# The S1·T1 product of a down projection by a second level of Strassen, with its right sums sharing a buffer through DRAM

## The chip, the cores and the metric

The kernel runs on one core of one Trainium2 chip. The metric is the device time of the whole program in microseconds, and the profile is one execution of it. TensorE (PE in the profile) does the matmuls, VectorE (DVE) the elementwise sums, ScalarE (ACT) copies, exponentials and the GELU, and SyncE (SP) issues the DMAs.

## The reference

Two blocks stand one after the other. The first is a cross attention between `x` (8 batches, 8 heads, 512 rows, 64 deep) and a `state` of 32 rows, in both directions. Its result is 544 rows of 512 numbers for each batch. The second is a two-layer net with a sigmoid GELU:

```python
scores = scale * x @ state.T;  a = softmax(scores);   xread = a @ state      # 512 rows
scores2 = scale * state @ x.T; a2 = softmax(scores2); sread = a2 @ x         # 32 rows
h = concat(xread, sread) @ w_in          # 512 -> 2048
g = h * sigmoid(1.702 * h)
return g @ w_out                          # 2048 -> 512
```

All is fp32.

## The kernel before, in words

**Batches and stages.** The 512 rows of xread are worked off batch by batch (b = 0 to 7). The 32 rows of sread of all batches come last, as one piece called "sr". Batch 0 uses plain matmuls. For b = 1 to 7 the down projection `g @ w_out` is done in `strassen_two(b, ...)`, and while it runs, the attention of batch b+1 is put between its products. That is done with hooks: `strassen_two` calls `hook("P2a")`, `hook("P6.3")` and so on at named points, and a dictionary says which pieces of other work are emitted there. Instructions are emitted by hand (`manual_schedule`), and every engine runs its own in the order of emission.

**The down projection.** `g` (512 tokens by 2048) and `w_out` (2048 by 512) are cut in halves in both directions and multiplied in seven products (Winograd's form of Strassen) in the order P1 = A11·B11, P2 = A12·B21, P5 = S1·T1, P6 = S2·T2, P3 = (A12−S2)·B22, P7 = S3·T3, P4 = A22·T4. The S are sums of quarters of `g`, and the T sums of quarters of `w_out`, made once. S1 and S2 lie in the tile `later`, T1, T2 and T4 in `sums`, T3 in place in `w_out`. One product is 256 tokens × 1024 × 256. Written plainly (`product` in `strassen_two`) it is 16 matmuls of 128×128 weights against 256 columns. An fp32 matmul shows as two records, so a product is 32 records.

**The second level.** Some of the seven are themselves done in seven products of quarters, by `strassen_low`: 7 products of 4 matmuls against 128 columns, 56 records. Before the change these are P6 and P7 (b = 1 to 7) and P4 (b = 2 to 7). `strassen_low` takes turns over three PSUM banks (`bank`, used as o[0], o[1], o[2], o[0], o[1], o[2], o[0]). After each product the result is added by DVE (the first copied by ACT) into `pu` or the target `R`, and `at(i)` lets other work in. A product can begin only when the instruction that emptied its bank is done. One bank is always `bank_o[1]`, where P2 is collected too. After P2, DVE empties `bank_o[1]` into `osb`, the output tile of the first quarter.

**What the second level needs.** On the right are three sums of quarters of T: `low2` and `low3` (for T2 and T3) lie in the tile `low`, those of T4 in DRAM, and are loaded into the x buffer each batch (`low4_load`). A further quarter of T is replaced in place (`low_third`). On the left are three sums of quarters of S and one replaced in place; for P6 these are three DVE instructions of 128×512 and a fourth (q1, q2, q4 and the line with `whole(1, 0)`).

**Buffers and helpers that the change touches.** `att_M(b, c)` computes a product of state and w_in, tile M of batch b, chunk c, and the four M tiles of a batch come from a pool with four turns. `up_sums(b)` makes sums of M for the up projection (`up_strassen`), which is called before P1 of the same batch and ends inside it. `att_s_norm` normalizes the second softmax. In the last batch (b = 7) there is no attention to prepare, so `sr_sums()` puts its DVE sums of w_in in the hooks instead: its `order` names how many at which hook.

Of the kernel before, what the change touches and what calls it, by code (L numbers as in the profile page):

```python
# [20 lines left out]
def kernel(  # L21
# [55 lines left out]
    konst = ctx.enter_context(tc.tile_pool(name="konst", bufs=1))  # L77
    xpool = ctx.enter_context(tc.tile_pool(name="xpool", bufs=1))
    apool = ctx.enter_context(tc.tile_pool(name="apool", bufs=1))
    mpool = ctx.enter_context(tc.tile_pool(name="mpool", bufs=4))  # L80
    gpool = ctx.enter_context(tc.tile_pool(name="gpool", bufs=1))
    opool = ctx.enter_context(tc.tile_pool(name="opool", bufs=1))
    dram = ctx.enter_context(tc.tile_pool(name="dram", bufs=1, space=bass.MemoryType.DRAM))
# [261 lines left out]
    def att_s_exp(b, room=None):  # L345
# [4 lines left out]
        for g in range(NG):  # L350
# [2 lines left out]
            nc.scalar.activation(out=e, in_=a["s"][g], func=AF.Exp, bias=a["mx2"][g], scale=scale, accum_out=sm)  # L353
            a["e2"].append((e, sm))

    def att_s_norm(b):

        for e, sm in A[b]["e2"]:
            nc.vector.tensor_scalar(sm, sm, eps, None, ALU.add)
            nc.vector.reciprocal(out=sm, in_=sm)  # L360
            nc.vector.tensor_scalar(e, e, sm, None, ALU.mult)

    NS1 = NG * NB

# [53 lines left out]
    def x_back(b, g):  # L418
# [2 lines left out]
            a["aT"] = apool.tile([P, NG, S], FP32, tag="aT", name=f"aT_{b}")  # L421
        nc.vector.transpose(a["aT"][:, g], a["e1"][:, g].rearrange("p i n -> p (i n)"))

    def att_M(b, c, spare=False):

        m = mpool.tile([P, NG, FC], FP32, tag="M", name=f"M_{b}_{c}")
        A[b]["M", c] = m
        name = f"M_{b}_{c}_"
        ps = [psH.tile([P, FC], FP32, tag="h", name=name + str(g)) if spare else att_ps([P, FC], name + str(g)) for g in range(NG)]
        by_state(b, ps, lambda rows, j: w_in[c][rows, j])  # L430
        for g in range(NG):
            nc.scalar.copy(m[:, g], ps[g])  # L432
# [150 lines left out]
    low2, low3 = ([low[:, 3 * i + k].rearrange("p (f n) -> p f n", f=QF) for k in range(3)] for i in range(2))  # L583


    kept4 = dram.tile([P, 3 * FC], FP32, name="low4")

    def low4_room():
        t = xpool.tile([P, SCH, H, D], FP32, tag="xn", name="low4")
        return t.rearrange("p c h d -> p (c h d)")[:, : 3 * FC]  # L590

    def low4_parts(t):
        return [t[:, FC * k : FC * (k + 1)].rearrange("p (f n) -> p f n", f=QF) for k in range(3)]

    def low4_make(a):
        t = low4_room()
        for fn, args in low_sums(T4, low4_parts(t)):
            fn(*args)
        nc.sync.dma_start(kept4, t)

    def low4_load(a):
        a["low4"] = low4_room()
        nc.sync.dma_start(a["low4"], kept4)

    def halves_of(t):

# [49 lines left out]

    def strassen_two(key, dst, hooks, a4):

        B11, B21, B22 = w_out[:, :HF, :HN], w_out[:, HF:, :HN], w_out[:, HF:, HN:]
        g = [G[key, u] for u in range(HF)]  # L660
        half = S // 2
# [30 lines left out]
            return [bank_o[1], *(psH.tile([P, FC], FP32, tag="h", name=f"low_{key}") for _ in range(2))]  # L692


        q1, q2, q4 = (g[i][:, :, :half].rearrange("p k (h t) -> p k h t", h=2) for i in range(3))
        v1, v2, v4 = (later[:, 1 + i].rearrange("p (k h t) -> p k h t", k=2, h=2) for i in range(3))
        k1 = g[3][:, :, :half]
        k2, k3, t01, o10, o01 = (room(i) for i in (0, 4, 5, 6, 7))
        z11, z12, z21, z22 = ([S2[:, QF * k + f, P * i : P * (i + 1)] for f in range(QF)] for i in range(2) for k in range(2))

        def whole(i, k):
            return S2[:, QF * k : QF * (k + 1), P * i : P * (i + 1)].rearrange("p (k h) t -> p k h t", h=2)

        def blocks(q):
            return [q[:, f // 2, f % 2] for f in range(QF)]

        product(bank(0), A_of(0, 0), B11, "P1")
        nc.scalar.copy(k1, bank(0))
        tt(q1, whole(1, 0), whole(1, 1))
        tt(q2, q1, whole(0, 0), ALU.subtract)  # L710
        tt(q4, whole(0, 1), q2, ALU.subtract)
        product(bank(1), A_of(0, 1), B21, "P2")
        osb = opool.tile([P, 2, HN], FP32, tag="osb", name=f"osb_{key}_00")
        tt(osb, bank(1), k1)
# [3 lines left out]
            a12 = quarters(key, NU + u, S)[0]  # L718
            tt(a12, a12, S2[:, 2 * u : 2 * u + 2, :half], ALU.subtract)

        for u in range(NU // 2):
            s4(u)
        tt(whole(1, 0), whole(0, 0), whole(1, 0), ALU.subtract)
        hook("P2")
        for u in range(NU // 2, NU):
            s4(u)
        hook("S4")
        product(bank(0), [S1[:, f, :half] for f in range(HF)], T1, "P5")
        b11, t3, b21, b22 = halves_of(T2)
        strassen_low(  # L730
            (z11, z12, z21, z22, blocks(q1), blocks(q2), blocks(q4)), (b11, t3, b21, b22, *low2),
            low_banks(), k2, lambda i: hook(f"P6.{i}"),
        )
        tt(k2, k2, k1)

        def sums(u0, rooms):

# [14 lines left out]
            return parts(0, 0), parts(1, 0), parts(0, 1), parts(1, 1), *(blocks(v) for v in rooms)  # L752

        left3 = sums(0, (v1, v2, v4))
        tt(t01, bank(0), k2)
        hook("P6")
        if a4 is not None:
            left4 = sums(NU, (q1, q2, q4))
        product(bank(3), A_of(0, 1), B22, "P3")
        b11, t3, b21, b22 = halves_of(T3)  # L760
        o, h0, h1 = low_banks()
        strassen_low(left3, (b11, t3, b21, b22, *low3), [h0, h1, o], k3, lambda i: hook(f"P7.{i}"))
        hook("P7")
        osb = opool.tile([P, 2, HN], FP32, tag="osb", name=f"osb_{key}_11")
        then = [
            lambda: tt(k3, k3, k2),
            lambda: tt(osb, bank(0), k3),
            lambda: out(1, 1, osb),
            lambda: tt(o01, bank(3), t01),
            lambda: out(0, 1, o01),  # L770
        ]
        if a4 is not None:
            turn = {1: then[:1], 2: then[1:3], 3: then[3:]}

            def at(i):
                for fn in turn.get(i, ()):
                    fn()
                hook(f"P4.{i}")

            b11, t3, b21, b22 = halves_of(T4)  # L780
            o, h0, h1 = low_banks()
            strassen_low(left4, (b11, t3, b21, b22, *low4_parts(a4["low4"])), [o, h1, h0], k1, at)
            p4 = k1
        else:
            for fn in then:
                fn()
            product(bank(2), A_of(1, 1), T4, "P4")
            for i in range(1, 8):
                hook(f"P4.{i}")
            p4 = bank(2)  # L790
# [4 lines left out]
    def hooks_next(b):  # L795

        h = {}

        def at(name, fn, *args):
            h.setdefault(name, []).append((fn, args))  # L800

        at("P1a", att_state, b)
        at("P1a", att_xT, b, 0)
        at("P1b", att_xT, b, 1)
        at("P1b", att_xT, b, 2)
        at("P1b", att_xT, b, 3, True)
        at("P2a", att_scores, b)
        at("P2a", att_M, b, 0)
        at("P2a", att_M, b, 1, True)
        at("P2a", att_blocks, b)  # L810
        at("P2a", att_s_max, b)
        at("P2a", att_s_exp, b)
        for g in range(NG):
            at("P2a", x_max, b, g)
            at("P2a", x_sub, b, g)
        at("P2a", x_exp, b)
        at("P2", att_s_norm, b)
        for name, fn, *args in (
            ("P6.1", x_sum, 0), ("P6.2", x_sum, 1), ("P6.3", x_inverse), ("P6.4", x_scale, 0), ("P6.6", x_scale, 1),
        ):  # L820
            at(name, fn, b, *args)
        for g in range(NG):
            at("P6", att_eT, b, g)
            at("P6", x_back, b, g)
        at("P3a", att_sread, b)
        at("P3a", att_M, b, 3, True)
        at("P3a", att_M, b, 2)
        steps = up_sums(b)
        for name, n in (("P3a", 7), ("P7.1", 1), ("P7.2", 1), ("P7.3", 1), ("P7.4", 1), ("P7.6", 1), ("P4.4", 2), ("P4.6", 1)):
            for fn, args in steps[:n]:  # L830
                at(name, fn, *args)
            steps = steps[n:]
        assert not steps
        at("P3b", att_srT, b)
        return h
# [56 lines left out]
    def sr_sums():  # L892

        HT, HK = B * Ns // 2, NPR // 2
        mm = [mpool.tile([P, NG, FC], FP32, tag="M", name=f"ws_{i}") for i in range(4)]
        s1, s2 = mm[:2], mm[2:]
        t = apool.tile([P, NPR, S], FP32, tag="xT", name="ws4")
        s4 = [t[:, HK * c : HK * (c + 1)] for c in range(2)]
        t = apool.tile([P, NG, NB, Ns], FP32, tag="e1", name="ta_sr").rearrange("p g i n -> p (g i n)")
# [8 lines left out]

        steps = []
        for c in range(2):  # L910
            steps.append((tt, (s1[c], hi[c][0], hi[c][1], ALU.add)))
            steps.append((tt, (s2[c], s1[c], lo[c][0])))
            steps.append((tt, (hi[c][0], lo[c][0], hi[c][0])))
            steps.append((tt, (s4[c], lo[c][1], s2[c])))
        steps += [(tt, v) for v in ((t1, r12, r11), (t2, r22, t1), (t3, r22, r12), (t4, r21, t2))]

        def each(v):
# [206 lines left out]
    for b in range(1, B):  # L1124
        if b > 1:
            ahead = {"P1a": [(up_strassen(b, S, *parts_x(b)), ())]}
        else:
            ahead = {
                "P1a": low_sums(T2, low2) + [(T_of, (T4, B21, T2)), (low_third, (T2,))],
                "P1b": low_sums(T3, low3) + [(low_third, (T3,))],  # L1130
            }
        if b + 1 < B:
            hooks = hooks_next(b + 1)
        else:

            steps, left, right = sr_sums()
            order = (
                ("P1b", 1), ("P2a", 4), ("P2", 1), ("P5a", 1), ("P3a", 1), ("P7.1", 1), ("P7.2", 1), ("P7.3", 1), ("P7.4", 1),
            )
            hooks = {}  # L1140
            for name, n in order:
                hooks[name], steps = steps[:n], steps[n:]
            assert not steps
            for name, t in (("P6", T2), ("P4.1", T3), ("P4.7", T4)):
                hooks[name] = [(low_third, (t,))]
        for name, first in ahead.items():
            hooks[name] = first + hooks.get(name, [])
        a4 = {}
        k = 3 if b + 1 < B else 0
        hooks["P3a"][k:k] = [(low4_load if b > 1 else low4_make, (a4,))]  # L1150
        strassen_two(b, out_of(b), hooks, a4 if b > 1 else None)
        if b == 1:
            low_third(T4)
# [38 lines left out]
```

## Time and profile before

| | |
|---|---|
| time | 735.43 us (median of 3, 735.40 to 735.52) |
| span of the profiled execution | 733.5 us, granted TensorE clock 0.999 |
| PE busy | 720.7 us, 98% of the span |
| DVE busy | 539.5 us, 74% |
| ACT busy | 234.1 us, 32% |
| DMA | 40.84 MB, mean 56 GB/s |

Busy time is the time in which an engine had an instruction running. The chain of waits, followed back from the last instruction, runs over PE for 95% of the span. Batches 2 to 6 look the same in the timeline, one every 79.4 us. Batch 1 and batch 7 differ from them, because batch 1 also makes the T sums, and batch 7 prepares no attention.

### The profile page before, as it was taken

What the parts mean: (1) busy time and instruction counts of PE and PEld (TensorE: products, weight loads), DVE (VectorE), ACT (ScalarE), POOL (GpSimd) and SP (SyncE); (2) the same over time, 40 slices, a digit from 0 to 9 for tenths busy, and PEclk for the clock granted to TensorE, in tenths of its full rate; (3) what the DMA queues carried; (4) which work ended last, traced back from release to release, by engine and by line L of the source; (5) the groups of instructions that cost most, each with busy time, mean ns of one, the idle gap of its engine ahead of it and who ended that gap; (6) DMA issues with size and microseconds to landing.
All of it is one profiled execution on the core that took longest, in us unless ns stands there. A gap on an engine that the chain in (4) does not pass through costs nothing.

```text
span 733.5 us, 11513 instructions
## 1 busy us (share of the span) xinstructions
PE 720.7 (98%) x4759; PEld 567.5 (77%) x4759; DVE 539.5 (74%) x1077; ACT 234.1 (32%) x430; POOL 0.8 (0%) x8
## 2 busy tenths in 40 slices
PE   7999999999999999999999999999999999999996
PEld 3333444467888789879888789878987988899995
DVE  6998999729856887668867786688766886788440
ACT  4786411033224511433144322451143314300210
POOL 0000000000000000000000000000000000000000
PEclk9999999999999999999999999999999999999999
DMA  8931245010140001300140014001130011010000
GB/s 225 355 91 54 90 154 135 0 59 15 44 105 1 16 31 57 61 1 16 45 104 1 16 45 105 0 16 35 54 62 1 15 44 44 1 57 30 16 1 29
DMA packets 49780, 40.84 MB, mean 56 GB/s; under 512 B 36544, under 2 KB 44224, under 8 KB 49728
## 3 DMA queue, kind: packets, MB, share of 16 engines
q1 hardware_dynamic: 49728, 40.11, 18.7%
q8 instruction: 37, 0.61, 0.4%
q14 instruction: 15, 0.12, 0.1%
HBM read 30.41 MB, written 9.70 MB: 55 GB/s over the span
## 4 chain that ended last, share of the span: by engine, by line
PE 95%; ACT 2%; DMA 2%; SPq 0%; DVE 0%; issue 0%; DVEq 0%; ACTq 0%
PE o L676 28%; PE o L944 17%; PE low L628 11%; PE o L490 8%; PE h L472 7%; PE o L628 6%; PE upx L944 6%; PE M L303 4%; PE o L533 2%; PE xT L282 2%; PE o L303 1%; PE sr L452 1%; PE warm L123 1%; PE upx_sr L944 1%; DMA out_dram<-osb_sr 1%; PE eT L441 1%
## 5 line engine op out<-in xcount | busy, mean ns | idle before, releaser
L676 PE MATMUL o<-w_out,g 128*128 128x256 f32 x672 | 152.7, 381 | 0.0
L954 DVE TENSOR_TENSOR g<-o,g 128x512 f32<-128x512 f32 (+1 forms) x140 | 88.1, 651 | 85.3 <-PE o L944 84.4
L676 PEld LDWEIGHTS o<-w_out,g 128*128 128x128 f32 x672 | 125.2, 190 | 26.2 <-issue 10.5
L951 ACT ACTIVATE g<-g 128x512 f32<-128x512 f32 (+1 forms) x84 | 49.9, 601 | 100.5 <-DVE g L954 100.5
L676 PE MATMUL o<-sums,later 128*128 128x256 f32 x224 | 49.5, 379 | 0.0
L944 PE MATMUL upx<-aT,M 128*128 128x256 f32 x192 | 49.3, 379 | 0.0
L944 PE MATMUL o<-ta,M 128*128 128x256 f32 x192 | 49.3, 379 | 0.0
L944 PE MATMUL o<-ta,ms 128*128 128x256 f32 x192 | 48.3, 379 | 0.0
L676 PEld LDWEIGHTS o<-sums,later 128*128 128x128 f32 x224 | 42.6, 190 | 5.8
L432 ACT COPY M<-M 128x512 f32<-128x512 f32 x64 | 33.2, 596 | 37.7 <-PE M L303 37.7
L944 PEld LDWEIGHTS o<-ta,ms 128*128 128x128 f32 x192 | 36.5, 190 | 5.0
L944 PEld LDWEIGHTS o<-ta,M 128*128 128x128 f32 x192 | 36.5, 190 | 5.0
L944 PEld LDWEIGHTS upx<-aT,M 128*128 128x128 f32 x192 | 36.1, 190 | 4.7
L513 DVE TENSOR_TENSOR later<-g,g 128x512 f32<-128x512 f32 (+1 forms) x32 | 20.8, 650 | 17.5 <-ACT g L475 17.5
L303 PE MATMUL M<-w_in,stT 64*32 64x512 f32 x512 | 32.7, 594 | 0.2 <-ACT eT L442 0.2
L628 PE MATMUL low<-low,g 128*128 128x128 f32 x256 | 32.8, 275 | 0.0
L472 PE MATMUL h<-low,M 128*128 128x512 f32 x64 | 29.7, 600 | 1.4 <-DVE low L384 1.4
L628 PEld LDWEIGHTS low<-low,g 128*128 128x128 f32 x256 | 30.7, 192 | 0.0
L472 PE MATMUL h<-aT,M 128*128 128x512 f32 x64 | 28.7, 599 | 1.4 <-ACT M L432 1.4
L635 ACT COPY pu<-o 128x128 f32<-128x128 f32 x13 | 3.5, 266 | 82.6 <-PE o L628 82.6
L490 PE MATMUL o<-w_out,g 128*128 128x512 f32 x64 | 28.7, 594 | 0.0
L490 PE MATMUL o<-w_out,sums 128*128 128x512 f32 x64 | 28.4, 594 | 0.0
(186 smaller groups left out, 1169.7 us busy)
## 6 DMA issues: line engine op xcount, KB each, us to landing
later<-in_moe_w_out_dram SPq DMA_DIRECT2D x16, 512.0 KB
xn<-in_x_dram SPq DMA_DIRECT2D x28, 256.0 KB
w_out<-in_moe_w_in_dram SPq DMA_DIRECT2D x12, 512.0 KB
low<-low SPq DMA_DIRECT2D x7, 768.0 KB
out_dram<-osb SPq DMA_DIRECT2D x18, 256.0 KB
out_dram<-later SPq DMA_DIRECT2D x14, 256.0 KB
later<-in_moe_w_in_dram SPq DMA_DIRECT2D x4, 512.0 KB
sums<-in_x_dram SPq DMA_DIRECT2D x4, 256.0 KB
```

Of the source, the lines that this page charges most:

```text
L282: nc.tensor.transpose(ps[:, c], x_heads(b, c, j), ident)
L303: nc.tensor.matmul(ps[g][st], A[b]["stT"][rows, st], rhs(rows, j), start=True, stop=True)
L432: nc.scalar.copy(m[:, g], ps[g])
L472: nc.tensor.matmul(hps, lhs[i], rhs[i], start=(i == 0), stop=(i == n - 1))
L490: nc.tensor.matmul(ops, G[key, f // 2][:, f % 2, P * r : P * (r + 1)], w_out[:, f], start=(f == 0), stop=(f == NF - 1))
L513: nc.vector.tensor_tensor(out=s1, in0=a21, in1=a22, op=ALU.add)
L533: nc.tensor.matmul(ps[:, r], lhs[f][:, P * r : P * (r + 1)], rhs[:, f], start=(first and r == 0 and f == 0), stop=(f == HF - 1), skip_grou ...
L628: nc.tensor.matmul(ps, lhs[f], rhs[:, f], start=(f == 0), stop=(f == QF - 1))
L676: nc.tensor.matmul(ps[:, r], lhs[f][:, P * r : P * (r + 1)], rhs[:, f], start=(r == 0 and f == 0), stop=(f == HF - 1), skip_group_check=True,)
L944: nc.tensor.matmul(ps[:, k], lhs[i][:, o : o + P], rhs[i], start=(first and k == 0 and i == 0), stop=(i == n - 1), skip_group_check=True,)
L951: nc.scalar.activation(out=dst, in_=src, func=AF.Gelu_apprx_sigmoid)
L954: nc.vector.tensor_tensor(out=dst, in0=ps, in1=x, op=ALU.add)
```

## The change

P5 is done by `strassen_low` as well in batches 2 to 7, so that four of the seven products use the second level. Its purpose is fewer PE cycles: 7 products of quarters in place of 8. Where its operands go:

- Left sums of S1: three rooms in the M tiles of chunks 2 and 3 (`spare_M`). These are idle between the end of the up projection and `att_M(b+1, 3)`. The fourth room holds the result p5, which then lies in SBUF and not in PSUM bank 0. The M tiles get fixed places by chunk (tags M0 to M3), with one buffer each.
- Right sums of T1: the place of `low3` is shared. `low_keep` writes the sums of T3 to DRAM in batch 1, `low5_make` makes those of T1 in the spare M rooms (hook "S4" of batch 1) and writes them to DRAM. From then on `low_load(3)` follows P5 and `low_load(5)` follows P7.
- DVE work moves: the three sums and the replaced quarter of S1 stand before P2. `s4(0)`, `s4(1)` and the replaced quarter of S2 go into P5's `at(1)` to `at(3)`. The normalizations of the second softmax go to `at(4)` and `at(6)` of P5. `t01` is formed right after P6.
- `sr_sums` can't use the M tiles of chunks 2 and 3 now, so it uses the tiles aT and eT, and its sums are cut in two (16 of 128×512 in place of 8 of 128×1024, and 4 small ones as before), with a new `order`. For "sr", T1 is restored by `low_third` in batch 7, as T2, T3 and T4 are.

```diff
+    turns = {"M": 0}
-        m = mpool.tile([P, NG, FC], FP32, tag="M", name=f"M_{b}_{c}")
+        m = mpool.tile([P, NG, FC], FP32, tag=f"M{turns['M'] % NFC if b < 2 else c}", name=f"M_{b}_{c}")
...
+    def low_load(k):
+        nc.sync.dma_start(turn_room, outside[k])
...
+    def spare_M():
+        m = [mpool.tile([P, NG, FC], FP32, tag=f"M{i}", name="spare_M") for i in (2, 3)]
+        return [v[:, g] for v in m for g in range(NG)]
+    def low5_make():
+        rooms = spare_M()
+        for fn, args in low_sums(T1, [v.rearrange("p (f n) -> p f n", f=QF) for v in rooms[:3]]):
+            fn(*args)
...
         product(bank(0), A_of(0, 0), B11, "P1")
         nc.scalar.copy(k1, bank(0))
-        tt(q1, whole(1, 0), whole(1, 1))
-        tt(q2, q1, whole(0, 0), ALU.subtract)
-        tt(q4, whole(0, 1), q2, ALU.subtract)
+        sums_of(S2, q1, q2, q4)
+        if not plain:
+            *r, p5 = spare_M()
...
+            sums_of(S1, *r)
+            third_of(S1)
         product(bank(1), A_of(0, 1), B21, "P2")
         osb = opool.tile([P, 2, HN], FP32, tag="osb", name=f"osb_{key}_00")
         tt(osb, bank(1), k1)
         out(0, 0, osb)
...
-        for u in range(NU // 2):
-            s4(u)
-        tt(whole(1, 0), whole(0, 0), whole(1, 0), ALU.subtract)
         hook("P2")
+        first = [lambda: s4(0), lambda: s4(1), lambda: third_of(S2)]
...
+            strassen_low(left_of(S1, *r), (b11, t3, b21, b22, *low5), [h0, h1, o], p5, at)
+            low_load(3)
         for u in range(NU // 2, NU):
             s4(u)
         hook("S4")
-        product(bank(0), [S1[:, f, :half] for f in range(HF)], T1, "P5")
+        if plain:
+            p5 = bank(0)
+            product(p5, [S1[:, f, :half] for f in range(HF)], T1, "P5")
...
-            low_banks(), k2, lambda i: hook(f"P6.{i}"),
+            left_of(S2, q1, q2, q4), (b11, t3, b21, b22, *low2), [h1, o, h0], k2, lambda i: hook(f"P6.{i}")
         tt(k2, k2, k1)
+        tt(t01, p5, k2)
...
+        if key + 1 < B:
+            low_load(5)
...
+        if b > 2:
+            at("P5.4", s_norm, b, 0)
+            at("P5.6", s_norm, b, 1)
+        else:
+            at("P2", att_s_norm, b)
...
+                steps += [(tt, (out[:, k], x0[:, k], x1[:, k], *op)) for k in range(HK)]
...
-            order = (
-                ("P1b", 1), ("P2a", 4), ("P2", 1), ("P5a", 1), ("P3a", 1), ("P7.1", 1), ("P7.2", 1), ("P7.3", 1), ("P7.4", 1),
-            )
+            order = [("P1b", 2), ("P2a", 8)]
+            order += [(name, 1) for name in ("P5.4", "P5.6", "P6.1", "P6.3", "P6.4", "P6.6", "P7.1", "P7.2", "P7.3", "P7.4")]
...
-            for name, t in (("P6", T2), ("P4.1", T3), ("P4.7", T4)):
+            for name, t in (("P6.2", T1), ("P6", T2), ("P4.1", T3), ("P4.7", T4)):
```

More of the change, by code (lines that the diff above doesn't have):

```diff
@@ L79 @@
     apool = ctx.enter_context(tc.tile_pool(name="apool", bufs=1))
-    mpool = ctx.enter_context(tc.tile_pool(name="mpool", bufs=4))
+    mpool = ctx.enter_context(tc.tile_pool(name="mpool", bufs=1))
     gpool = ctx.enter_context(tc.tile_pool(name="gpool", bufs=1))
@@ L354, in att_s_exp, with s_norm @@
             a["e2"].append((e, sm))
+    def s_norm(b, g):
+        e, sm = A[b]["e2"][g]
+        nc.vector.tensor_scalar(sm, sm, eps, None, ALU.add)
+        nc.vector.reciprocal(out=sm, in_=sm)
+        nc.vector.tensor_scalar(e, e, sm, None, ALU.mult)
     def att_s_norm(b):
[L358 to L361, printed above, removed]
+        for g in range(NG):
+            s_norm(b, g)
     NS1 = NG * NB
@@ L422, in x_back @@
         nc.vector.transpose(a["aT"][:, g], a["e1"][:, g].rearrange("p i n -> p (i n)"))
+    turns = {"M": 0}
     def att_M(b, c, spare=False):
-        m = mpool.tile([P, NG, FC], FP32, tag="M", name=f"M_{b}_{c}")
+        m = mpool.tile([P, NG, FC], FP32, tag=f"M{turns['M'] % NFC if b < 2 else c}", name=f"M_{b}_{c}")
+        turns["M"] += 1
         A[b]["M", c] = m
@@ L583, with low_keep @@
     low2, low3 = ([low[:, 3 * i + k].rearrange("p (f n) -> p f n", f=QF) for k in range(3)] for i in range(2))
-    kept4 = dram.tile([P, 3 * FC], FP32, name="low4")
+    low5 = low3
+    outside = {k: dram.tile([P, 3 * FC], FP32, name=f"low_{k}") for k in (3, 4, 5)}
+    turn_room = low[:, 3:].rearrange("p k n -> p (k n)")
+    def low_load(k):
+        nc.sync.dma_start(turn_room, outside[k])
+    def low_keep(k, src):
+        nc.sync.dma_start(outside[k], src)
     def low4_room():
@@ L590, in low4_room, with low_parts @@
         return t.rearrange("p c h d -> p (c h d)")[:, : 3 * FC]
-    def low4_parts(t):
+    def low_parts(t):
         return [t[:, FC * k : FC * (k + 1)].rearrange("p (f n) -> p f n", f=QF) for k in range(3)]
@@ L596, in low4_make @@
         t = low4_room()
-        for fn, args in low_sums(T4, low4_parts(t)):
+        for fn, args in low_sums(T4, low_parts(t)):
             fn(*args)
-        nc.sync.dma_start(kept4, t)
+        low_keep(4, t)
     def low4_load(a):
         a["low4"] = low4_room()
-        nc.sync.dma_start(a["low4"], kept4)
+        nc.sync.dma_start(a["low4"], outside[4])
+    def spare_M():
[5 more added lines that the diff above has]
+            fn(*args)
+        for k in range(3):
+            nc.sync.dma_start(outside[5][:, FC * k : FC * (k + 1)], rooms[k])
     def halves_of(t):
@@ L657, in strassen_two @@
     def strassen_two(key, dst, hooks, a4):
+        plain = a4 is None
         B11, B21, B22 = w_out[:, :HF, :HN], w_out[:, HF:, :HN], w_out[:, HF:, HN:]
@@ L698, in strassen_two, with whole, sums_of, third_of @@
         k2, k3, t01, o10, o01 = (room(i) for i in (0, 4, 5, 6, 7))
-        z11, z12, z21, z22 = ([S2[:, QF * k + f, P * i : P * (i + 1)] for f in range(QF)] for i in range(2) for k in range(2))
-        def whole(i, k):
-            return S2[:, QF * k : QF * (k + 1), P * i : P * (i + 1)].rearrange("p (k h) t -> p k h t", h=2)
+        def whole(s, i, k):
+            return s[:, QF * k : QF * (k + 1), P * i : P * (i + 1)].rearrange("p (k h) t -> p k h t", h=2)
         def blocks(q):
             return [q[:, f // 2, f % 2] for f in range(QF)]
+        def sums_of(s, r1, r2, r4):
+            tt(r1, whole(s, 1, 0), whole(s, 1, 1))
+            tt(r2, r1, whole(s, 0, 0), ALU.subtract)
+            tt(r4, whole(s, 0, 1), r2, ALU.subtract)
+        def third_of(s):
+            tt(whole(s, 1, 0), whole(s, 0, 0), whole(s, 1, 0), ALU.subtract)
+        def left_of(s, *rooms):
+            z = [[s[:, QF * k + f, P * i : P * (i + 1)] for f in range(QF)] for i in range(2) for k in range(2)]
+            return *z, *(blocks(v) for v in rooms)
         product(bank(0), A_of(0, 0), B11, "P1")
         nc.scalar.copy(k1, bank(0))
-        tt(q1, whole(1, 0), whole(1, 1))
-        tt(q2, q1, whole(0, 0), ALU.subtract)
-        tt(q4, whole(0, 1), q2, ALU.subtract)
+        sums_of(S2, q1, q2, q4)
+        if not plain:
+            *r, p5 = spare_M()
+            r = [v.rearrange("p (k h t) -> p k h t", k=2, h=2) for v in r]
+            p5 = p5.rearrange("p (r n) -> p r n", r=2)
+            sums_of(S1, *r)
+            third_of(S1)
         product(bank(1), A_of(0, 1), B21, "P2")
@@ L719, in s4, with at @@
             tt(a12, a12, S2[:, 2 * u : 2 * u + 2, :half], ALU.subtract)
-        for u in range(NU // 2):
-            s4(u)
-        tt(whole(1, 0), whole(0, 0), whole(1, 0), ALU.subtract)
         hook("P2")
+        first = [lambda: s4(0), lambda: s4(1), lambda: third_of(S2)]
+        if plain:
+            for fn in first:
+                fn()
+        else:
+            def at(i):
+                for fn in first[i - 1 : i]:
+                    fn()
+                hook(f"P5.{i}")
+            b11, t3, b21, b22 = halves_of(T1)
+            o, h0, h1 = low_banks()
+            strassen_low(left_of(S1, *r), (b11, t3, b21, b22, *low5), [h0, h1, o], p5, at)
+            low_load(3)
         for u in range(NU // 2, NU):
@@ L727, in strassen_two @@
         hook("S4")
-        product(bank(0), [S1[:, f, :half] for f in range(HF)], T1, "P5")
+        if plain:
+            p5 = bank(0)
+            product(p5, [S1[:, f, :half] for f in range(HF)], T1, "P5")
         b11, t3, b21, b22 = halves_of(T2)
+        o, h0, h1 = low_banks()
         strassen_low(
-            (z11, z12, z21, z22, blocks(q1), blocks(q2), blocks(q4)), (b11, t3, b21, b22, *low2),
-            low_banks(), k2, lambda i: hook(f"P6.{i}"),
+            left_of(S2, q1, q2, q4), (b11, t3, b21, b22, *low2), [h1, o, h0], k2, lambda i: hook(f"P6.{i}")
         )
         tt(k2, k2, k1)
+        tt(t01, p5, k2)
         def sums(u0, rooms):
@@ L754, in strassen_two @@
         left3 = sums(0, (v1, v2, v4))
-        tt(t01, bank(0), k2)
         hook("P6")
-        if a4 is not None:
+        if not plain:
             left4 = sums(NU, (q1, q2, q4))
@@ L765, in strassen_two @@
         then = [
+            lambda: tt(osb, k3, t01),
+            lambda: out(1, 1, osb),
             lambda: tt(k3, k3, k2),
-            lambda: tt(osb, bank(0), k3),
-            lambda: out(1, 1, osb),
             lambda: tt(o01, bank(3), t01),
@@ L771, in strassen_two @@
         ]
-        if a4 is not None:
-            turn = {1: then[:1], 2: then[1:3], 3: then[3:]}
+        if not plain:
+            turn = {1: then[:2], 2: then[2:3], 3: then[3:]}
             def at(i):
@@ L781, in strassen_two @@
             o, h0, h1 = low_banks()
-            strassen_low(left4, (b11, t3, b21, b22, *low4_parts(a4["low4"])), [o, h1, h0], k1, at)
+            strassen_low(left4, (b11, t3, b21, b22, *low_parts(a4["low4"])), [o, h1, h0], k1, at)
             p4 = k1
@@ L816, in hooks_next @@
         at("P2a", x_exp, b)
-        at("P2", att_s_norm, b)
+        if b > 2:
+            at("P5.4", s_norm, b, 0)
+            at("P5.6", s_norm, b, 1)
+        else:
+            at("P2", att_s_norm, b)
         for name, fn, *args in (
@@ L894, in sr_sums @@
         HT, HK = B * Ns // 2, NPR // 2
-        mm = [mpool.tile([P, NG, FC], FP32, tag="M", name=f"ws_{i}") for i in range(4)]
-        s1, s2 = mm[:2], mm[2:]
+        s1 = [mpool.tile([P, NG, FC], FP32, tag=f"M{i}", name=f"ws1_{i}") for i in range(2)]
+        s2 = [apool.tile([P, NG, S], FP32, tag="aT", name="ws2_0")]
+        t = apool.tile([P, NG, SCH, P], FP32, tag="eT", name="ws2_1")
+        s2.append(t.rearrange("p g c q -> p g (c q)"))
         t = apool.tile([P, NPR, S], FP32, tag="xT", name="ws4")
@@ L910, in sr_sums @@
         for c in range(2):
[L911 to L914, printed above, removed]
+            for out, x0, x1, *op in (
+                (s1[c], hi[c][0], hi[c][1], ALU.add),
+                (s2[c], s1[c], lo[c][0]),
+                (hi[c][0], lo[c][0], hi[c][0]),
+                (s4[c], lo[c][1], s2[c]),
+            ):
+                steps += [(tt, (out[:, k], x0[:, k], x1[:, k], *op)) for k in range(HK)]
         steps += [(tt, v) for v in ((t1, r12, r11), (t2, r22, t1), (t3, r22, r12), (t4, r21, t2))]
@@ L1129 @@
                 "P1a": low_sums(T2, low2) + [(T_of, (T4, B21, T2)), (low_third, (T2,))],
-                "P1b": low_sums(T3, low3) + [(low_third, (T3,))],
+                "P1b": low_sums(T3, low3) + [(low_keep, (3, turn_room)), (low_third, (T3,))],
+                "S4": [(low5_make, ())],
+                "P7.5": [(low_third, (T1,))],
             }
@@ L1149 @@
         k = 3 if b + 1 < B else 0
-        hooks["P3a"][k:k] = [(low4_load if b > 1 else low4_make, (a4,))]
+        hooks.setdefault("P3a", [])[k:k] = [(low4_load if b > 1 else low4_make, (a4,))]
         strassen_two(b, out_of(b), hooks, a4 if b > 1 else None)
```

## The prediction

> **What bounds the kernel now.** I read the page first (busy shares and the chain of waits), then the timeline of one batch of each kind around P5, then the DMA share by stretches. The page says that PE is the bound almost everywhere:
>
> ```profile
> PE 720.7 (98%) x4759; PEld 567.5 (77%) x4759; DVE 539.5 (74%) x1077; ACT 234.1 (32%) x430; POOL 0.8 (0%) x8
> ...
> PE 95%; ACT 2%; DMA 2%; SPq 0%; DVE 0%; issue 0%; DVEq 0%; ACTq 0%
> ```
>
> So PE time saved counts in full, unless a wait comes in its place. P5 will now wait for DVE, and 74% is only a mean, so DVE's place at P5 must be read in each kind of batch. Batch 3 stands for 2 to 6 (start, duration, engine and line):
>
> ```profile
> 325.21 0.69 DVE L683 TENSOR_TENSOR g<-later,g 128x512 f32<-128x512 f32 x1
> 327.82 1.31 DVE L334 STREAM_TRANSPOSE e<-o 128x512 f32<-128x512 f32 x2 [1.92 <-PE o L303]
> 332.91 7.07 PE L676 MATMUL o<-sums,later 128*128 128x256 f32 x32
> 333.24 0.68 DVE L683 TENSOR_TENSOR osb<-o,g 128x512 f32<-128x512 f32 x1
> 333.36 1.06 ACT L400 ACTIVATE e<-e 128x1024 f32<-128x1024 f32 x1
> 339.81 1.05 PE L628 MATMUL o<-sums,later 128*128 128x128 f32 x8
> 341.60 1.06 PE L628 MATMUL low<-sums,later 128*128 128x128 f32 x8
> ```
>
> P5 is the third line and P6 begins at 339.81, so P5 costs 339.81 − 332.91 = 6.90 us. Products 1 and 3 of P6 begin 1.79 apart, so a quarter product costs 0.893 us. DVE sits idle for 1.92 us between the last sum of S2 (first line) and the score transposes, and it empties P2's bank into `osb` 0.33 us after P5 has begun. Batch 7, with no attention to wait for:
>
> ```profile
> 641.40 1.22 DVE L907 TENSOR_TENSOR ws<-w_in 128x1024 f32<-128x1024 f32 x1
> 642.54 0.68 DVE L683 TENSOR_TENSOR g<-later 128x512 f32<-128x512 f32 x1
> 643.33 0.69 DVE L683 TENSOR_TENSOR g<-g,later 128x512 f32<-128x512 f32 x1
> 644.12 0.69 DVE L683 TENSOR_TENSOR g<-later,g 128x512 f32<-128x512 f32 x1
> 644.73 1.22 DVE L907 TENSOR_TENSOR ws<-ws,w_in 128x1024 f32<-128x1024 f32 x1
> 645.89 7.07 PE L676 MATMUL o<-sums,later 128*128 128x256 f32 x32
> 649.27 0.68 DVE L683 TENSOR_TENSOR osb<-o,g 128x512 f32<-128x512 f32 x1
> 652.80 1.05 PE L628 MATMUL o<-sums,later 128*128 128x128 f32 x8
> ```
>
> Here DVE is behind already: `osb` starts 3.38 us after P5, with no idle time ahead of it. P5 as it is uses bank 0, so nobody waits. Batch 1, in P6:
>
> ```profile
> 182.66 0.68 DVE L406 TENSOR_REDUCE sm<-e 128x16 f32<-128x512 f32 x1
> 183.26 0.28 DVE L631 TENSOR_TENSOR pu<-low,pu 128x128 f32<-128x128 f32 x1
> 183.84 1.06 PE L628 MATMUL low<-low,g 128*128 128x128 f32 x8
> ```
>
> The second line empties the bank of product 2, and product 5 (third line) takes that bank 0.3 us later, so DVE has hardly any slack there.
>
> [...] This trace shows the FIFO in batch 7, where `osb` stands behind four `ws` sums although its own input is long done. So what the change emits ahead of `osb` delays it.
>
> In the timeline an independent 128×512 instruction follows the last one after 0.61 us (644.12 to 644.73) and one that reads the last one's result after 0.79 (642.54 to 643.33). I use these spacings.
>
> **PE, batches 2 to 7.** P5 goes from 6.90 us to 7 × 0.893 = 6.25. That saves 0.65 us a batch, 3.9 us over six.
>
> **The new wait.** P5's product 3 uses `bank_o[1]`, so it waits for `osb`. Nominally it starts 1.79 us after P5. Behind it on PE stand all other products.
>
> **Batches 2 to 6.** Ahead of the transposes stand four more DVE instructions (r1, r2, r4 and the quarter of S1). From r1 at 325.82: +0.79, +0.79, +0.61, +0.61, so the transposes start at 328.62 and not 327.82. The 1.92 us of idle time hides all but 0.80. Everything up to `osb` slides by 0.80, and `osb` ends at 333.24 + 0.80 + 0.68 = 334.72. Product 3 is due at 332.91 + 1.79 = 334.70. The wait is 0.02 us plus the passing of the signal, which I put at 0.1 to 0.2 in all. The exponential on ACT (333.36) slides too and ends at 335.2, and the copy of product 1's result stands behind it until 335.5. Product 4 needs that bank at 334.8 + 0.89 = 335.7, just in time. Then DVE has in P5 seven adds (about 0.25 each), `s4` twice and the quarter of S2 (3 × 0.61) and two normalizations (0.78 each): about 5.1 us in 6.25, each add two products ahead of the reuse of its bank. No wait follows. After P6 the sums for P3 and P7 begin where they did, and DVE had 1.39 us idle before P7's first add. Moving `t01` forward costs nothing there. Net gain 0.65 − 0.15 = 0.5 a batch (bounds 0.1 and 0.65), 2.5 us over five.
>
> **Batch 7.** DVE is continuous from 641.40. In the new order come two halves of ws (2 × 0.61, to 642.62), q1, q2, q4 (0.79 + 0.79 + 0.61, to 644.81), r1, r2, r4 and the quarter (2.80, to 647.61), and eight halves of ws at hook P2a (8 × 0.61, to 652.5). Only then comes `osb`, which ends at 653.2. Product 3 is due at 645.89 + 1.79 = 647.68, so PE stands for 5.5 us. From there DVE has about 4.6 us of work (5 × 0.61 and seven adds) against 4.5 us of PE in the last five products, each add two products ahead of the reuse of its bank, and keeps up. P6 also carries four halves of ws and the restoring of T1 (0.61 each), which fit between its adds, two products ahead of each bank's reuse. The rest of the batch is a row of PE work with no idle time that could give this back. Cost 5.5 − 0.65 = 4.9 us (bounds 4.2 and 5.6).
>
> **Batch 1.** `low5_make` puts three dependent sums (0.79 + 0.71 + 0.61 = 2.1 us, as the same three take at low2) ahead of P6's adds. The add at 183.26 ends at 185.64 instead of 183.54, and product 5, due at 183.84, waits 1.8 us (bounds 1.2 and 2.2). The next adds slide by the same and meet their banks. DVE stays about 0.3 us further behind, and 2.27 us of idle time before P7 takes that up. Restoring in P7.5 (0.7 us) falls where nothing waits.
>
> **DMA.** Each batch adds two loads of 768 KB. The same load in the kernel before (`low4_load`, issued at 351.65) reads so in stretches, with the last column in GB/s:
>
> ```profile
> 353.00:354.00 1.00, 1.00 (x17) 0.56 (x4) 0.97 (x4) 1.00 (x3) 0.00 (x0) 1.00 0.80 264
> 354.00:355.00 1.00, 1.00 (x6) 0.88 (x5) 1.00 (x4) 0.75 (x2) 0.00 (x0) 1.00 0.89 369
> 355.00:356.00 1.00, 1.00 (x6) 0.89 (x5) 0.97 (x4) 0.00 (x0) 0.00 (x0) 1.00 0.24 98
> ```
>
> It is over 4 us after the issue. `low_load(3)` is issued after P5's product 6, at about 338.5, and P7's product 2 reads it at 357.9. `low_load(5)` has over 40 us. Both are hidden.
>
> **Sum.** 735.43 − 2.5 + 4.9 + 1.8 = 739.6 us.
>
> **Rivals.** (a) The waits do not appear, because DVE turns out to have room: 735.4 − 3.9 = 731.5 us, faster. For it speak the 74% and the idle time in batches 2 to 6. Against it speaks batch 7, where DVE has none. (b) In batches 2 to 6 the slid exponential makes product 4 wait as well, or the signal is slow, and the gain is nothing: 735.4 + 4.9 + 1.8 = 742.1. For it, the margin there is only 0.2 us. Against it, ACT and DVE are within reach in every step. (c) The waits in batches 1 and 7 are half of what I work out, because sums overlap more: the waits are 0.9 and 2.75, so −3.9 + 3.65 + 0.5 for the signal gives 735.7, no change. (d) The loads from DRAM come late for P7: one microsecond a batch more gives 745. The idle DMA between 338.7 and 352 speaks against it.
>
> **Chances.** The forecast 0.76, (a) 0.08, (b) 0.08, (c) 0.05, (d) 0.03. So faster 0.08, within 0.2% (734.0 to 736.9) 0.06, slower 0.86. The bounds of the three terms give 735.4 + 1.2 + 4.2 − 3.25 = 737.6 and 735.4 + 2.2 + 5.6 − 0.5 = 742.7. With (b) inside and (a), (c), (d) outside I give 737.0 to 742.5.
>
> **What would show it.** In batch 7 PE stands for 5.5 us before the third quarter product of P5, with `osb` as what ended the wait. In batch 1 it stands 1.8 us before product 5 of P6, with a `pu` add. In batches 2 to 6 P5's start and P6's start are 6.3 to 6.5 us apart, and no DMA ends a PE wait after the start. I am wrong if PE has no idle time in batch 7, or if batches 2 to 6 lose more than 0.65 us.

## The result, and the profile after

| | before | after |
|---|---|---|
| time (median) | 735.47 us (735.40 to 735.52, 4 runs) | 741.13 us (740.57 to 741.84, 4 runs) |
| ratio | | 1.0078, 95% interval 1.006 to 1.0095 |
| span of the profiled execution | 733.5 us | 738.7 us |

The change makes the kernel slower by 5.7 us. First, the page of the changed kernel: busy shares, and the chain of waits.

```profile
PE 719.8 (97%) x4903; PEld 570.6 (77%) x4903; DVE 566.5 (77%) x1156; ACT 235.5 (32%) x436; POOL 0.8 (0%) x8
...
PE 90%; DVE 5%; ACT 2%; DMA 2%; issue 1%; SPq 0%; DVEq 0%; ACTq 0%
```

PE has hardly less busy time (719.8 against 720.7). It has 144 more matmul records, because P5 now shows as 56 short ones in place of 32 longer ones in six batches, and the 3.9 us that this should save are mostly not there. DVE, which had 0% of the chain, now holds 5% of it. (The chain counts all DVE work that leads up to a wait, so its share does not measure the loss: in the first experiment below it is 7%, in a faster kernel.) The list of who waited for whom on PE says where (total us, times, longest):

```profile
PE o L656 <- DVE osb L713: 5.2, 1, 5.2
PE o L656 <- DVE pu L659: 1.6, 1, 1.6
```

Two waits, each once in the whole run, are new. In the timeline the first lies in batch 7. L656 is the quarter product, L975 a half of the ws sums, and L713 the sums of S1 and S2 and `osb`:

```profile
645.49 1.06 PE L656 MATMUL low<-low,spare_M 128*128 128x128 f32 x8
645.56 0.68 DVE L713 TENSOR_TENSOR later<-later 128x512 f32<-128x512 f32 x1
...
646.16 1.28 DVE L975 TENSOR_TENSOR ws<-ws,w_in 128x512 f32<-128x512 f32 x2
647.37 1.28 DVE L975 TENSOR_TENSOR w_in<-w_in,w_in 128x512 f32<-128x512 f32 x2
648.57 1.28 DVE L975 TENSOR_TENSOR ws<-w_in,ws 128x512 f32<-128x512 f32 x2
649.77 1.28 DVE L975 TENSOR_TENSOR ws<-w_in 128x512 f32<-128x512 f32 x2
650.98 0.68 DVE L713 TENSOR_TENSOR osb<-o,g 128x512 f32<-128x512 f32 x1
...
651.71 1.98 PE L656 MATMUL o<-sums,later 128*128 128x128 f32 x8 [5.17 <-DVE osb L713]
```

The reader sees product 2 of P5 at 645.49, DVE without a gap in the sums, `osb` behind the eighth, and product 3 the moment `osb` is done. What I had not seen coming is the duration 1.98. Stretches of the same profile (stretch, its length, busy PE, PEld, DVE, ACT, POOL, then the granted clock, where 1.00 is full speed, the DMA share and GB/s):

```profile
646.00:649.00 3.00, 0.55 (x5) 0.35 (x4) 3.00 (x6) 0.00 (x0) 0.00 (x0) 1.00 0.00 0
649.00:651.70 2.70, 0.00 (x0) 0.00 (x0) 2.70 (x6) 0.00 (x0) 0.00 (x0) 1.00 0.00 0
651.70:653.50 1.80, 1.79 (x9) 1.79 (x10) 1.36 (x3) 0.00 (x0) 0.00 (x0) 0.54 0.43 146
653.50:655.20 1.70, 1.70 (x10) 1.70 (x9) 0.89 (x2) 0.00 (x0) 0.00 (x0) 0.50 0.00 0
655.20:657.00 1.80, 1.80 (x17) 1.80 (x17) 1.38 (x4) 0.00 (x0) 0.00 (x0) 0.99 0.00 0
```

After the wait PE is busy for 3.5 us at half the clock, so in that time it does the work of 1.75: products 3 and 4 take 655.20 − 651.71 = 3.49 us in place of 1.79, which loses 1.70. The second wait lies in batch 1:

```profile
182.58 0.68 DVE L1157 TENSOR_TENSOR spare_M<-sums 128x512 f32<-128x512 f32 x1
...
183.30 1.42 DVE L1157 TENSOR_TENSOR spare_M<-sums,spare_M 128x512 f32<-128x512 f32 x2
...
185.23 0.28 DVE L659 TENSOR_TENSOR pu<-o,pu 128x128 f32<-128x128 f32 x1
...
185.56 1.16 PE L656 MATMUL o<-low,g 128*128 128x128 f32 x8 [1.60 <-DVE pu L659]
```

The three sums of `low5_make` stand ahead of the add, and product 5 waits for it. Batch 3 shows the gain as it was meant:

```profile
329.67 1.30 DVE L334 STREAM_TRANSPOSE e<-o 128x512 f32<-128x512 f32 x2
...
334.11 1.05 PE L656 MATMUL low<-sums,later 128*128 128x128 f32 x8
...
335.08 0.68 DVE L713 TENSOR_TENSOR osb<-o,g 128x512 f32<-128x512 f32 x1
...
335.89 1.08 PE L656 MATMUL o<-sums,later 128*128 128x128 f32 x8
...
340.38 1.06 PE L656 MATMUL low<-sums,later 128*128 128x128 f32 x8
```

The idle time ahead of the transposes is gone. `osb` ends at 335.76, and product 3 starts at 335.89, 1.78 after the first. From P5 to P6 it takes 340.38 − 334.11 = 6.27 us instead of 6.90.

**The account.** From the start of P1 in batch 2 to that in batch 3 it was 312.57 − 233.13 = 79.44 us and is now 313.77 − 234.95 = 78.82, so 0.62 us a batch are gained, 3.1 over batches 2 to 6. In batch 1, from P6 to P3, it was 7.12 and is 8.99: 1.87 lost. In batch 7, from P5 to P3, it was 13.16 and is 19.56: 6.40 lost. The parts of these 6.40 are product 3, which starts 5.32 us after its due time (644.60 + 1.79), and the 1.70 of slow products, less the 0.65 that PE saves, together 6.37. The sum over all batches is +5.2 us, the difference of the spans.

### The profile page after: what moved, and what is told of

It reads as the page before. It is cut to its first block, busy times and chain, and to the rows that moved or that the text cites. A ratio compares the mean times of both kernels' runs of the same rounds, so it can differ in the third digit from the quotient of the medians.

```text
span 738.7 us, 11929 instructions
## 1 busy us (share of the span) xinstructions
PE 719.8 (97%) x4903; PEld 570.6 (77%) x4903; DVE 566.5 (77%) x1156; ACT 235.5 (32%) x436; POOL 0.8 (0%) x8
## 4 chain that ended last, share of the span: by engine, by line
PE 90%; DVE 5%; ACT 2%; DMA 2%; issue 1%; SPq 0%; DVEq 0%; ACTq 0%
PE o L706 19%; PE o L1015 16%; PE low L656 14%; PE o L497 7%; PE o L656 7%; PE h L479 7%; PE upx L1015 6%; PE M L303 4%; PE o L540 2%; PE xT L282 2%; PE o L303 1%; PE sr L459 1%; PE warm L123 1%; PE upx_sr L1015 1%; DMA out_dram<-osb_sr 1%; DVE g L713 1%
## 5 line engine op out<-in xcount | busy, mean ns | idle before, releaser
L656 PE MATMUL low<-sums,later 128*128 128x128 f32 x264 | 34.6, 279 | 0.0
L656 PEld LDWEIGHTS low<-sums,later 128*128 128x128 f32 x264 | 33.0, 196 | 0.4
L1033 ACT COPY g<-upx 128x512 f32<-128x512 f32 x24 | 13.7, 572 | 42.4 <-PE upx L1015 42.4
L482 ACT ACTIVATE g<-h 128x512 f32<-128x512 f32 x24 | 14.0, 592 | 40.5 <-PE h L479 40.5
L479 PEld LDWEIGHTS h<-aT,M 128*128 128x128 f32 x64 | 11.8, 190 | 18.3 <-issue 12.2
```

What stands on the lines that cost most here:

```text
L479: nc.tensor.matmul(hps, lhs[i], rhs[i], start=(i == 0), stop=(i == n - 1))
L656: nc.tensor.matmul(ps, lhs[f], rhs[:, f], start=(f == 0), stop=(f == QF - 1))
```

## The experiments

**The sums of batch 7, spread.** Is it their place on DVE, or is the second level dearer than it looks?

```diff
-            order = [("P1b", 2), ("P2a", 8)]
-            order += [(name, 1) for name in ("P5.4", "P5.6", "P6.1", "P6.3", "P6.4", "P6.6", "P7.1", "P7.2", "P7.3", "P7.4")]
+            order = [("P1b", 2)]
+            order += [(f"P5.{i}", 1) for i in (4, 5, 6, 7)] + [(f"P6.{i}", 1) for i in (1, 3, 4, 5, 6, 7)]
+            order += [(f"P7.{i}", 1) for i in (1, 2, 3, 4, 5, 6)] + [("P4.4", 1), ("P4.6", 1)]
```

> The changed kernel, but in batch 7 the eight sums of hook P2a go one by one into P5, P6, P7 and P4. Theory A (most of the loss is that osb stands behind these sums on DVE, so PE waits 5.2 us, and the granted clock halves after so long a wait): the wait before product 3 of P5 falls from 5.2 to about 0.5 us, no stretch of batch 7 has a clock below 0.99, and the time falls by about 6.5 us to some 734.3. Theory B (the sums of S1, the two added DMAs a batch or the moved sums themselves cost PE, and the wait only happens to be there): the time stays above 738, or the same wait turns up at another product of batch 7.

Measured: 734.74 us, ratio to before 0.999 (0.9982 to 0.9998). This is the batch's third quarter product:

```profile
646.25 0.68 DVE L713 TENSOR_TENSOR osb<-o,g 128x512 f32<-128x512 f32 x1
...
646.99 1.16 PE L656 MATMUL o<-sums,later 128*128 128x128 f32 x8 [0.36 <-DVE osb L713]
```

The same work in another order is 6.4 us faster. The wait is 0.36 us, and the clock is 1.00 throughout the batch's P5 and P6. Theory B falls as an account of the loss. The 0.4 us that are missing against the expectation are mostly in P7, from 664.72 to 671.25: 6.53 us, against 7 × 0.893 = 6.25. Sums now stand among its adds on DVE.

**Another bank for P5.** Is it the shared bank, or DVE's queue?

```diff
-            strassen_low(left_of(S1, *r), (b11, t3, b21, b22, *low5), [h0, h1, o], p5, at)
+            strassen_low(left_of(S1, *r), (b11, t3, b21, b22, *low5), [h0, h1, bank_o[0]], p5, at)
```

> The changed kernel, but P5's third bank is bank_o[0], which nobody holds, in place of bank_o[1], which osb must empty first; DVE's order stays. Theory A1 (what counts is DVE's place in its queue, whatever bank it is): product 3 and 4 of P5 in batch 7 start at once, and product 5 waits some 4.3 us for the add of product 2, which stands behind the same sums: the time falls by about 1 us, to 740. Theory A2 (the shared bank is the cause): no wait is left in P5, and the time falls by 6 to 7 us, to 734.5.

Measured: 740.22 us (ratio 1.0067, 1.0053 to 1.008). The waits on PE:

```profile
PE low L656 <- DVE pu L659: 4.2, 1, 4.2
PE o L656 <- DVE pu L659: 1.6, 1, 1.6
```

The wait moved from `osb` to the next add in the queue, from product 3 to product 5, and fell by 1 us. A1 holds for this change alone: freeing the bank alone does little, for every later add stands behind the same sums.

**Matmuls in the gap.** What makes the products after the wait slow?

```diff
+    nought = konst.tile([P, FC], mybir.dt.bfloat16, name="nought")
+    nc.vector.memset(nought, 0.0)
...
+                if key == B - 1 and i == 2:
+                    for _ in range(22):
+                        nc.tensor.matmul(bank_o[2], nought[:, :P], nought, start=True, stop=True)
```

> The changed kernel, with 22 bf16 matmuls of 128x512 of zeros into an unused bank between products 2 and 3 of P5 in batch 7 (about 4.7 us, less than the wait of 5.2). Nothing else changes. Theory C (the half clock after the wait, 0.54 and 0.50 between 651.7 and 655.2, comes from PE standing idle): osb and product 3 start at the same time as before, but the clock stays near 1.0 and the time falls by 1.7 to 2.3 us, to about 739. Theory D (the slow matmuls after the wait come from what runs beside them: osb's store, DVE's reads of the same tiles): products 3 to 5 remain at 1.7 to 1.8 us each and the time stays at 741.

Measured: 739.47 us (ratio 1.0055, 1.0042 to 1.0068), 1.7 us less than the changed kernel. The timeline and then the clock by stretches:

```profile
646.88 4.70 PE L779 MATMUL o<-nought 128*128 128x512 bf16 x21
...
651.27 0.68 DVE L715 TENSOR_TENSOR osb<-o,g 128x512 f32<-128x512 f32 x1
...
652.01 1.16 PE L658 MATMUL o<-sums,later 128*128 128x128 f32 x8 [0.43 <-DVE osb L715]
```

```profile
652.00:654.00 2.00, 1.99 (x17) 2.00 (x18) 2.00 (x5) 0.00 (x0) 0.00 (x0) 1.00 0.39 131
654.00:656.00 2.00, 2.00 (x20) 2.00 (x19) 1.59 (x6) 0.00 (x0) 0.00 (x0) 1.00 0.00 0
```

One of the 22 records is missing from the trace. Product 3 still waits for `osb` at the same place, 652.01 − 644.88 = 7.13 us after P5 began (7.11 in the changed kernel), and the same DVE work and the same store run beside it. But PE did not stand idle, the clock stays at 1.00, and product 3 takes 1.16 and not 1.98. Theory D falls.

**Half of the sums at P2a.** How long must PE stand for the clock to fall?

```diff
-            order = [("P1b", 2), ("P2a", 8)]
-            order += [(name, 1) for name in ("P5.4", "P5.6", "P6.1", "P6.3", "P6.4", "P6.6", "P7.1", "P7.2", "P7.3", "P7.4")]
+            order = [("P1b", 2), ("P2a", 4)]
+            order += [(f"P5.{i}", 1) for i in (4, 6)] + [(f"P6.{i}", 1) for i in (1, 3, 4, 5, 6, 7)]
+            order += [(f"P7.{i}", 1) for i in (1, 2, 3, 4)] + [("P4.4", 1), ("P4.6", 1)]
```

> The changed kernel, but only four of the eight sums stay at P2a, the others are spread over P5 to P4. Theory C (half clock only after an idle stretch as long as 5 us): the wait is about 2.75 us, the clock stays above 0.95, the time falls by 2.4 us of wait and about 2 us of slow matmuls, to 736.7. Theory L (loss in proportion to the wait, slow matmuls included): half the loss remains, about 737.9, with slow matmuls after the wait as before.

Measured: 738.40 us (ratio 1.0037, 1.0024 to 1.0049). Four of the five runs took 738.24 to 738.53 with a mean clock of 0.997, and one 736.93 with 0.999. The profiled one is of the four:

```profile
649.51 2.07 PE L656 MATMUL o<-sums,later 128*128 128x128 f32 x8 [2.77 <-DVE osb L713]
...
651.37 1.82 PE L656 MATMUL low<-sums,later 128*128 128x128 f32 x8
...
653.03 1.06 PE L656 MATMUL low<-low,spare_M 128*128 128x128 f32 x8
```

The wait is as long as expected. Products 3 and 4 are slow all the same, so the part of theory C that wants an idle stretch as long as 5 us falls: 2.77 us are enough, mostly. Theory L is right that slow matmuls remain, but not that they shrink with the wait: they lose 653.03 − 649.51 − 1.79 = 1.73 us, against 1.70 after the longer wait. The run at 736.93 fits what C expected without the fall, but it has no profile. The wait of 1.60 us in batch 1 does not bring it about: from 185.5 on the clock there is 1.00.

**How long the half clock lasts.** The profile of the other bank and that of the next experiment have a long wait in batch 7 as well, and they show what the changed kernel's own profile hides. With the other bank, where PE stands from 648.23 to 652.42:

```profile
648.00:650.00 2.00, 0.23 (x3) 0.04 (x1) 2.00 (x4) 0.00 (x0) 0.00 (x0) 1.00 0.00 0
650.00:652.00 2.00, 0.00 (x0) 0.00 (x0) 2.00 (x4) 0.00 (x0) 0.00 (x0) 0.65 0.00 0
652.00:654.00 2.00, 1.58 (x7) 1.58 (x8) 2.00 (x7) 0.00 (x0) 0.00 (x0) 0.50 0.39 131
654.00:656.00 2.00, 2.00 (x12) 2.00 (x10) 1.02 (x3) 0.00 (x0) 0.00 (x0) 0.50 0.00 0
656.00:658.00 2.00, 2.00 (x13) 2.00 (x13) 1.12 (x4) 0.00 (x0) 0.00 (x0) 0.65 0.27 77
```

Here the clock falls in the middle of the wait. Stretches of 0.2 us give the times in all four profiles (us; "lost" is what the slow products took beyond 0.893 each):

| profile | PE stops | clock falls | clock is back | at half | lost |
|---|---|---|---|---|---|
| changed kernel | 646.55 | 651.8 | 655.2 | 3.4 | 1.70 |
| half of the sums | 646.75 | 649.6 | 653.0 | 3.4 | 1.73 |
| `low5_make` early | 644.73 | 647.2 | 654.0 | 6.8 | 2.03 |
| another bank | 648.23 | 650.6 | 657.4 | 6.8 | 2.47 |

The clock fell 2.4 to 5.3 us after PE had stopped, and it stayed at half for 3.4 or 6.8 us. Half clock inside the wait costs nothing: with the other bank 1.8 of the 6.8 us lay inside it, and the 5.0 behind it account for the 2.47 lost. So the loss depends on when the clock falls, and not only on the length of the wait. What decides that moment these four profiles don't show.

**`low5_make` ahead of batch 1.**

```diff
+    low5_make()
     s12(1, NU - 1, S)
     s3(1, NU - 1, S)
...
-                "S4": [(low5_make, ())],
```

> The changed kernel, but low5_make is emitted ahead of batch 1, before the last s12, where DVE stood idle for 14 us. Theory A (the three sums ahead of P6's adds make PE wait 1.6 us in batch 1, and P6 takes 8.99 us in place of 7.12): no PE wait on pu in batch 1, P6 to P3 7.1 us again, the time falls by 1.9 us to about 739.2. Theory B (batch 1 is slower because of the stores to DRAM that it adds): the wait goes but P6 to P7 stays about 2 us longer than before the change, and the time stays at 741.

Measured: 739.00 us (ratio 1.0049, 1.0036 to 1.0063), 2.1 us less than the changed kernel. The start of P6 and of P3:

```profile
180.25 1.05 PE L656 MATMUL low<-sums,later 128*128 128x128 f32 x8
...
187.37 3.62 PE L706 MATMUL o<-w_out,g 128*128 128x256 f32 x16
```

The wait on `pu` is gone, and from P6 to P3 it is 187.37 − 180.25 = 7.12 us, as before the change. Theory A holds. The added stores cost this stage nothing.

**Batch 7's P5 as it was.** P5 is plain in batch 7 alone, while the eight sums stay where the change put them. (Two of the later sums move to hooks of the plain P5, and batch 6 no longer loads the sums of T1.)

```diff
+        flat5 = plain or key == B - 1
...
-        if plain:
-            p5 = bank(0)
+        if flat5:
+            p5 = bank(0)
...
-            for name, t in (("P6.2", T1), ("P6", T2), ("P4.1", T3), ("P4.7", T4)):
+            for name, t in (("P1a", T1), ("P6", T2), ("P4.1", T3), ("P4.7", T4)):
```

> The changed kernel, but batch 7 does P5 plainly as before the change (bank 0, no sums of S1, T1 restored at P1a), with the eight sums left at P2a. Theory A (batch 7 loses by the second level only because its product 3 needs the bank that osb empties): osb is as late as before, some 4 us after P5 starts, but nobody waits, and the time is 735.46 - 5 x 0.62 + 1.9 = about 734.2. Theory B (batch 7 is slower because of the DVE sums at P2a as such): a wait of several us stays in P6, and the time is above 737.

Measured: 734.02 us (ratio 0.9981, 0.9974 to 0.9988). P5 and `osb`:

```profile
644.72 7.07 PE L707 MATMUL o<-sums,later 128*128 128x256 f32 x32
...
649.05 0.68 DVE L714 TENSOR_TENSOR osb<-o,g 128x512 f32<-128x512 f32 x1
```

`osb` starts at 649.05, 4.3 us after P5, and nobody waits for it. So the queue of DVE alone does no harm. It needs a PE instruction that asks for its end.

**All three edits.** The sums spread (with the four small ones at P4.4 to P4.6, so that P7.5 and P7.6 stay free), bank 0, and `low5_make` early.

> The changed kernel with three edits at once: batch 7's eight sums of P2a spread over P5 to P4, P5's third bank bank_o[0], low5_make ahead of batch 1. Theory A (the second level gains 0.62 us a batch, and all else are waits that can be placed elsewhere): no wait on osb or pu over 0.1 us, and the gain in six batches shows in full: 735.46 - 6 x 0.62 = 731.7 us. Theory B (the 768 KB loads and the added DVE work cost time of their own): at least 1 us of the gain is missing, 732.7 or more, with PE waiting somewhere else.

Measured: 732.23 us (732.06 to 732.25), ratio to before 0.9956 (0.9944 to 0.9969). It beats both kernels: 3.2 us faster than before the change, 8.9 us faster than with it. No new wait of PE appears in the list. A period of batches 2 to 6 is now 78.79 us, so 0.65 us a batch are gained, all that PE saves. Against 731.7 some 0.5 us are missing. Batch 7 holds 0.4 of them: P5 and P6 take 642.64 to 655.32, which is 12.68 us and not 14 × 0.893 = 12.50, and P7 takes 6.49 and not 6.25; some products there start a little late. That is short of the 1 us that theory B wanted. The last 0.1 was not traced. So even in this order the second level saves batch 7 only 0.24 us of the 0.65 (from P5 to P4 it takes 26.08 us, before the change 26.32). The gain comes from the five batches in the middle. A kernel with P5 plain in batch 7 and `low5_make` early should do about as well: 734.02 less the 1.87 of batch 1 is 732.2, an estimate that was not run.

## Why the prediction was right

The direction, the places and the order of the terms came out as argued, and 741.13 lies in the range of 737.0 to 742.5. It is 1.5 us above the forecast of 739.6. Part of the closeness is luck: the cost of batch 7 lay outside its own bounds, and a gain in batches 2 to 6 that was larger than forecast took back 0.6 us of it.

- **PE, 0.65 us a batch.** Right: 6.90 became 6.27.
- **Batches 2 to 6, net 0.5 us.** The right sign, a little too small: 0.62. I had put 0.1 to 0.2 us on the passing of the signal, an estimate with no trace behind it, but product 3 started within 0.02 us of its due time, as DVE's spacing came out a little shorter: the four added instructions took 2.66 us (327.01 to 329.67) and not 2.80.
- **Batch 7, a wait of 5.5 us before product 3, ended by `osb`.** Right, with 5.17 of idle time, or 5.32 counted from the due time as the forecast did. The step that failed is the one after it, "Cost 5.5 − 0.65 = 4.9 us" with bounds of 4.2 and 5.6: it let PE go on at full speed. The batch lost 6.40, because PE ran at half the clock for 3.5 us after the wait and lost 1.70 by it. The matmuls in the gap showed that the idle stretch is the cause of the half clock: with them it stayed at 1.00, without them it was 0.50 to 0.54. I had not asked what 5 us of standing still do to the clock. (The 4.6 us of DVE work behind `osb` are 4.8 with the 0.25 us per add used elsewhere. PE did not wait for `osb` or an add again in P5 and P6, so nothing hung on it.)
- **Batch 1, 1.8 us.** Right: a wait of 1.60, or 1.76 counted from the due time of product 5, and 1.87 over the stage.
- **DMA hidden.** Right: no PE wait in batches 1 to 7 is ended by a load of right sums.
- **Rivals.** (a) and (c) fell with the waits, (b) with the 0.62, and (d) with the hidden loads.

In sum: −3.1 + 1.87 + 6.40 = +5.2 in the profiled run. That run has the highest clock of the four (0.997, the others 0.993 to 0.995), and the median is 0.5 us above it. The slower three have no profile. The same wait with a half clock of 6.8 us lost 2.03 in another kernel, 0.3 more than the 1.70 here, so a fall of the clock at another moment is the likely cause, but it is not shown for these runs.

## What to carry to other kernels

When PE is handed smaller products that turn over their banks faster, count for every bank which instruction empties it and what stands ahead of that one in its engine's queue, in the first and the last batch too, where the mix of work differs. Two stalls in two of seven batches ate a gain that was there in five. The place of DVE work ahead of a PE-critical drain is worth more than its amount: moving the same sums took 6.4 us off the time. When a wait can't be avoided, price the clock after it as well, not only the wait: here 1.7 to 2.5 us more. And ask of each batch by itself whether the change pays there.

## What the runs showed of the hardware that was not expected

- A wait of 5.17 us on PE was followed by 3.5 us at a granted clock of 0.50 to 0.54. One of 2.77 us was followed by half clock in the profiled run, and in four of five runs by the mean clock and time (738.2 to 738.5 against 736.9). One of 1.60 us was not: the clock after it was 1.00. The clock fell 2.4, 2.5 and 2.9 us after PE had stopped in three profiles, and 5.3 us after it in the fourth.
- The clock stayed at half for 3.4 us in two profiles and for 6.8 us in two others. The loss was 1.70 to 2.47 us and did not follow the length of the wait (1.73 after 2.77 us, 1.70 after 5.17).
- Plain bf16 matmuls of zeros in the gap held the clock at 1.00 and took 1.7 us off the time, though they do no useful work.
- Kernels in which the clock fell also scatter more: over 1.3 us for the changed kernel (740.57 to 741.84) and 1.6 for half of the sums, but 0.5 with the matmuls in the gap and 0.2 with all three edits.
